# A new order for the first steps of a retention and gated feed-forward kernel, with filler products and two held-back loads

## The chip, the cores and the metric

The kernel runs on one core of a Trainium2 chip. The metric is the device time of one execution in microseconds (us); the runs are repeated, and the median counts. Smaller is better.

## What is computed

The reference has two parts in sequence, all in float32:

```python
# q, k, v: (B=4, H=8, S=768, D=64); gamma: one constant per head
for t in range(S):
    state = gamma * state + outer(k[:, :, t], v[:, :, t])      # (B, H, D, D)
    y[:, :, t] = (1 / sqrt(D)) * q[:, :, t] @ state
x = y.transpose(0, 2, 1, 3).reshape(3072, 512)
h = x @ w_in                                                   # (512, 2048)
g = h * sigmoid(1.702 * h)
out = g @ w_out                                                # (2048, 512)
```

The kernel receives both weights as pairs of 32-bit words of 64-bit numbers, and narrows them to float32 by itself. Reading them so is part of its work, and most of the early work of VectorE.

## The kernel before, in words

**Attention.** The recurrence is done in chunks of 64 positions, for two batch entries at a time, so that there are 24 steps; the first eight (`2 * CB`) are written out in a list together with the first feed-forward block. For step j:

- `load` (L125 to L164) fetches q, k and v of the chunk. Steps 0 to 5 fetch them in plain form and turn them on TensorE. q and v come by SP's queue; k comes by the engine that the argument at L150 chooses: ACT for step 0, POOL for the others. q, k and v have two buffers each.
- `turn` (L241) makes eight transposes on TensorE (L250, four of q and four of k) into two PSUM tiles, and `turned` (L258) has ACT copy them to SBUF (L261).
- `decay` (L263) has ACT scale k by the decay within the chunk, one head at a time (L272, eight instructions).
- `attend` (L281) has two halves. Written `stepJ`, it makes the 16 products of k and q of step j (L289), into the tile `pa`. Written `step-F`, it makes the products of step f that need them: 16 of decayed k and v (L297, the addition to the state), 16 of the old state and q (L306, not for step 0), 16 of the masked product and v (L312). `pa` has one buffer, so the next `stepJ` waits until `masked` and `updated` have read it.
- `masked` (L316, L318) multiplies by the decay mask on VectorE. `by_state` ("state", L325), `output` ("x", L347, or L349 on ACT for a first chunk), `aged` (L357, ACT) and `updated` (L366 or L368, VectorE) make the output X and the new state.

**Feed-forward.** `up0` (L407) is a unit of 16 products of 128x128 by 128x256 in two groups of eight (L414; each product is seen twice in the profile[...]). "up0.T.P" takes the half T of the first block of positions and the P-th pair of columns of w_in. It needs X of steps 2T and 2T+1 and the P-th narrowed weights. "gate" is ACT's activation (L393) of the result.

**Narrowing.** `fetch` (L178) reads half a pair of columns, 512 KB, into one of three raw buffers by SP's queue (L180). `Narrow.start` ("abs", ACT, L207), `half` (three VectorE instructions, L211 to L213) and `rest` (three more, L217, L218, L222) make float32 of it. Weights 0 are done in two parts, 0a and 0b, and the others in one part of 1024 columns. A raw buffer is free after `rest`.

**Order.** A planner does not decide here. The list of names at the end (L944 to L962) is the program's order, and `pin` keeps it so on each engine: every name emits its instructions to its engines in the order of the list. Each engine runs in order and waits by semaphores. A DMA of SP's queue also waits for the one eight places before it to land. `begin` (L841) fetches small constants by POOL and makes the identity; `rows` (L859) and "mask" (L901) make the decay mask, and `causal` (L864) has POOL cut it to a triangle. `keep_warm` ("warm", L854) is a product of the identity by itself, 512 columns, into the spare PSUM tile `idle`. `lay_rowd` (L869) and `lay_whole` (L874) lay out more constants.

After the list comes the rest of the kernel: the blocks of positions after the first two, and the output products. The change does not touch it.

Of the kernel before, what the change touches and what calls it, by code (L numbers as in the profile page):

```python
# [9 lines left out]
F32 = mybir.dt.float32  # L10
# [3 lines left out]
P = 128  # L14
# [14 lines left out]
def kernel(  # L29
# [29 lines left out]
    pe, act, dve, pool, sp = nc.tensor, nc.scalar, nc.vector, nc.gpsimd, nc.sync  # L59
    ctx.enter_context(tc.manual_schedule(engines={mybir.EngineType.PE}))  # L60

    B, H, S, D = q.shape
    NT, DM = out.shape
    DFF = moe_w_in.shape[1]
    HP = H // 2
# [17 lines left out]
    ps_a = ctx.enter_context(tc.tile_pool(name="ps_a", bufs=1, space=bass.MemoryType.PSUM))  # L83
# [17 lines left out]
    rowd = const.tile([P, HP, D], F32, name="rowd")  # L101
# [3 lines left out]
    whole = const.tile([P, HP], F32, name="whole")  # L105
    whole_h = const.tile([P, H], F32, name="whole_h")
    ident = const.tile([P, P], F32, name="ident")
    mask = const.tile([P, 2, HP, D], F32, name="mask")
# [9 lines left out]
    def pin(i):  # L118
        return tc.keep_in_program_order(i) if ordered[0] else i
# [5 lines left out]
    def load(j, what="qkv"):  # L125

        b, c = j // NC * 2, j % NC
        rows = slice(c * D, (c + 1) * D)  # L130
        keep = tc.keep_in_program_order if j < 2 * CB else lambda i: i

        def plain(name, src, tag, bufs, engine=sp):
            t = two.tile([P, H, D], F32, name=name + "_in", tag=tag, bufs=bufs)
            QKV[name, j] = t
            for i in range(2):
                if j < NEW:
                    to, at = t[i * D:(i + 1) * D], src[b + i, :, rows, :].rearrange("h p d -> p h d")
                    for n in range(1 if name == "v" else 2):
                        keep(engine.dma_start(*((to, at) if name == "v" else (to[:, n:H:2], at[:, n * HP:(n + 1) * HP]))))  # L140
                else:
                    for r in range(2):
                        keep(engine.dma_start(t[r * D:(r + 1) * D, i * HP:(i + 1) * HP],
                                              src[b + i, r * HP:(r + 1) * HP, rows, :].rearrange("h p d -> p h d")))

        if j < NEW:
            if "q" in what:
                plain("q", q, "q_sq", 2)
            if "k" in what:
                plain("kn", k, "k_sq" if j in (0, 1, 4, 5) else "o", 2, pool if j else act)  # L150
        elif "q" in what:
            for name, src in (("q", q), ("k", k)):
                t = two.tile([P, H, D // C4, C4], F32, name=name + "_sq")
                for r0 in range(0, P, C4):
                    for n in range(D // C4):
                        t0 = c * D + n * C4
                        tc.keep_in_program_order(sp.dma_start(
                            t[r0:r0 + C4, :, n], src[b + r0 // D, :, t0:t0 + C4, r0 % D:r0 % D + C4]
                            .rearrange("h p d -> p h d")))
                QKV[name, j] = t  # L160
        if "v" in what:
            if j >= NEW and c < NC - 1:
                plain("kn", k, "kn", 1)
            plain("v", v, "v", 2)  # L164
# [4 lines left out]
    RAWS = [r.rearrange("p a b -> p (a b)").bitcast(U32)  # L169
            for r in (W2[:, 4], W2[:, 5], G[:, 6:8].rearrange("p a s t -> p a (s t)"))]  # L170
# [11 lines left out]
    class Narrow:  # L182
# [30 lines left out]
            pin(dve.scalar_tensor_tensor(hi, hi, 0x80000000, mu, op0=ALU.bitwise_and, op1=ALU.bitwise_or))  # L213

        def rest(self):
            m, mu, lo, hi = self.m, self.mu, self.lo, self.hi
            pin(dve.tensor_scalar(mu, hi, 0xFF800000, None, op0=ALU.bitwise_and))  # L217
            pin(dve.scalar_tensor_tensor(lo.bitcast(F32), lo, 2.0 ** -52, m, op0=ALU.mult, op1=ALU.mult))  # L218
            a, b = lo.bitcast(F32), hi.bitcast(F32)
            if self.i < NFF:  # L220
                a, b = [t.rearrange("p (c ab f) -> p c ab f", ab=2, f=P) for t in (a, b)]
            pin(dve.tensor_add(self.w, b, a))  # L222
# [4 lines left out]
    QT, KT, KD, AT, TURNED, PA, PU, PY, SHARE = [{} for _ in range(9)]  # L227
    HALF = [slice(i * D, (i + 1) * D) for i in range(2)]
    TWO = [(i, r) for i in range(2) for r in range(2)]
# [11 lines left out]
    def turn(j):  # L241

        QT[j], KT[j] = home(j, "qT"), home(j, "kT")
        if j < NEW:

            x = QKV.pop(("q", j)), QKV["kn", j]
            TURNED[j] = p = [ps.tile([P, HP, P], F32, name="pt", tag="y") for i in range(2)]
            for n in (1, 0) if j else (0, 1):
                for s in range(HP):
                    pe.matmul(p[n][:, s, :], x[n][:, 2 * s:2 * s + 2].rearrange("p r d -> p (r d)"), ident, is_transpose=True)  # L250
        else:
            for t, name in ((QT[j], "q"), (KT[j], "k")):
                tc.keep_in_program_order(dve.transpose(
                    t.rearrange("p h t -> p (h t)"), QKV.pop((name, j)).rearrange("p h n d -> p (h n d)")))
        if 2 * CB <= j < NCH - 2:
            load(j + 2, "qk")
# [386 lines left out]
    def down49(m, ring, comps):  # L643
# [25 lines left out]
        def home2(name, first, rest):  # L669
            kept[name] = first.rearrange("p (j e) -> p j e", e=P), rest[:, 0:3 * P].rearrange("p (j e) -> p j e", e=P)  # L670
            return kept[name]
# [167 lines left out]
    first = const.tile([P, 1], F32, name="first")  # L839
    idle = ps.tile([P, 4 * P], F32, name="idle", tag="x")  # L840
    works, products = {}, {}  # L841
# [12 lines left out]
    def keep_warm():  # L854

        pe.matmul(idle.rearrange("p (a b) -> p a b", a=4), ident, ident[:, None, :].to_broadcast([P, 4, P]),
                  start=True, stop=True)

    def rows():  # L859

        products["rows"] = p = ps.tile([P, H, D], F32, name="rows", tag="x")
        pe.matmul(p.rearrange("p h t -> p (h t)"), ones, row.rearrange("p h t -> p (h t)"), start=True, stop=True)
# [22 lines left out]
    def halves_anew():  # L885
# [14 lines left out]

        "mask": lambda: pin(dve.tensor_mul(m3, products["rows"], cold[:, 0:H, None].to_broadcast([P, H, D]))),  # L901
        "causal": causal, "rows": rows,
        "rowd": lay_rowd, "whole": lay_whole, "late_loads": late_loads, "anew": halves_anew,
        "warm": keep_warm}
    for j in range(2 * CB):
        for name in "qkv":
            works[f"{name}{j}"] = lambda j=j, name=name: load(j, name)
# [13 lines left out]
        works[f"w{i // 2}{'ab'[i % 2]}"] = lambda i=i: fetch(i)  # L921
    for name, i in [("0a", 0), ("0b", 1)] + [(str(p), 2 * p) for p in range(1, NFF)]:
        n = Narrow(i)
        works |= {"abs" + name: n.start, "half" + name: n.half, "rest" + name: n.rest}

    units = [0]

# [14 lines left out]

    begin()
    for name in """  # L944
        k0 table q0 warm turn0 w0b rows warm k1 abs0b q1 turned0 step0 v0 w0a half0b mask k2 turn1 causal rest0b
        masked0 decay0 v1 decay1 abs0a half0a step-0 updated0 turned1 q2 step1 rowd whole w2b turn2 w2a x0 k3
        aged1 masked1 turned2 v2 rest0a abs2 q3 step-1 updated1 state1 decay2 aged2 step2 q4 x1 half2 decay3 w3b
        w3a up0.0.0 masked2 turn3 k4 step-2 v3 q5 rest2 k5 gate0.0.0 turned3 updated2 state2 step3 up0.0.2
        masked3 abs3 half3 x2 rest3 turn4 w1b step-3 aged3 gate0.0.2 turned4 state3 w1a w5b updated3 v5 decay4
        abs1 x3 turn5 half1 up0.0.3 turned5 up0.1.2 step4 aged4 w5a rest1 v4 gate0.0.3 decay5 w6a masked4  # L950
        gate0.1.2 abs5 w6b step5-4 half5 rest5 up0.0.1 updated4 abs6 state4 gate0.0.1 w4b
        up0.1.1 half6 aged5 w4a up0.0.5 rest6 masked5 up0.1.5 gate0.1.1 x4 gate0.0.5 abs4 step-5 w8b w8a
        half4 gate0.1.5 state5 updated5 anew q6 up0.1.6 x5 rest4 gate0.1.6 abs8 v6 decay6 aged6 up0.0.6 w7b w7a half8
        turn6 gate0.0.6 up0.1.0 abs7 seven_4.2 seven_6.2 half7 gate0.1.0 w9b w9a up0.1.4 q7 gate0.1.4 step6 masked6 rest7 up0.0.4 v7
        gate0.0.4 seven_52.2 turn7 up0.1.3 gate0.1.3 step7-6 seven_4.0 masked7 updated6 decay7 aged7 abs9 state6 x6 up0.0.7 rest8 seven_w.0 gate0.0.7
        w11a w11b step-7 state7 x7 seven_x half9 w10b w10a up0.1.7 gate0.1.7
        seven2.0 seven2.1 abs11 rest9 seven2.2 seven_v.0 w12a w12b seven2.3 half11 seven2.4 abs10 seven_4.1 seven_w.1
        seven2.5 rest11 seven2.6 w14b w14a seven0.0 seven0.1 half10 seven0.2 abs12 seven0.3 rest10 w13a w13b seven0.4
        seven_v.1 seven0.5 seven_4.3 half12 seven_w.3 seven0.6 seven1.0 abs14 seven1.1 rest12 w15a w15b seven1.2 seven1.3
        half14 seven1.4 abs13 seven_v.3 seven1.5 updated7 rest14 seven1.6 seven3.0 seven3.1 half13 seven3.2 abs15 seven3.3  # L960
        rest13 seven3.4 seven3.5 late_loads half15 rest15 seven3.6 seven_end
    """.split():  # L962
        works[name]()
# [94 lines left out]
```

## Time and profile before

| | before |
|---|---|
| median of three runs, us | 661.88 (661.77 to 662.99) |
| the profiled execution, us | 662.24 |
| its span in the profile, us | 660.5 |
| mean granted clock of TensorE | 0.997 |
| TensorE busy with products, us | 642.2 (97%) |
| TensorE busy with weight loads, us | 580.2 (88%) |
| VectorE busy, us | 453.9 (69%) |
| ScalarE (ACT) busy, us | 159.0 (24%) |
| GpSimd (POOL) busy, us | 198.8 (30%) |

The span runs from the first to the last instruction of the program; the time of an execution is 1.74 us more in the profiled one. Shares of the span are averages over stages with different limits: the part that the list writes out runs to about 160 us, and attention steps 0 to 5 lie in its first 75 us. Times below are counted from the span's start. In a line of the timeline the first number is the start, the second the length of a group of instructions, in brackets stands the idle time before it and what ended it.

### The profile page before, as it was taken

What the parts mean: (1) busy time and instruction counts of PE and PEld (TensorE: products, weight loads), DVE (VectorE), ACT (ScalarE), POOL (GpSimd) and SP (SyncE); (2) the same over time, 40 slices, a digit from 0 to 9 for tenths busy, and PEclk for the clock granted to TensorE, in tenths of its full rate; (3) what the DMA queues carried; (4) which work ended last, traced back from release to release, by engine and by line L of the source; (5) the groups of instructions that cost most, each with busy time, mean ns of one, the idle gap of its engine ahead of it and who ended that gap; (6) DMA issues with size and microseconds to landing.
All of it is one profiled execution on the core that took longest, in us unless ns stands there. A gap on an engine that the chain in (4) does not pass through costs nothing.

```text
span 660.5 us, 15291 instructions
## 1 busy us (share of the span) xinstructions
PE 642.2 (97%) x6390; PEld 580.2 (88%) x6390; DVE 453.9 (69%) x645; ACT 159.0 (24%) x306; POOL 198.8 (30%) x225
## 2 busy tenths in 40 slices
PE   6789999999999999999999999999999999999997
PEld 3778888888788888889999888999888999988997
DVE  3699989999936973556984445995354995254965
ACT  4674233551000000333100233010233110233110
POOL 6400311310379217000536400445600255500000
PEclk9989999999999999999999999999999999999999
DMA  9995549763233556262485832386742252602142
GB/s 176 193 274 173 152 104 241 172 163 60 49 82 135 137 149 153 58 248 96 118 199 134 279 57 97 86 223 135 225 118 97 66 154 104 235 21 96 55 154 96
DMA packets 148149, 91.86 MB, mean 139 GB/s; under 512 B 131600, under 2 KB 134416, under 8 KB 147056
## 3 DMA queue, kind: packets, MB, share of 16 engines
q1 hardware_dynamic: 135856, 45.19, 29.8%
q0 software_dynamic: 9888, 44.46, 20.6%
q10 hardware_dynamic: 2336, 1.25, 0.6%
q8 instruction: 50, 0.82, 0.5%
q14 instruction: 19, 0.16, 0.1%
HBM read 72.89 MB, written 15.47 MB: 134 GB/s over the span
## 4 chain that ended last, share of the span: by engine, by line
PE 89%; DVE 4%; DMA 4%; SPq 1%; issue 1%; ACT 0%; DVEq 0%
PE pq L666 27%; PE px L562 17%; PE pd L799 13%; PE py L562 13%; PE ph L491 7%; PE ph L414 5%; PE pa L289 2%; PE py L312 2%; PE pa L297 2%; PE py L306 2%; DMA W<-in_moe_w_in_dram 1%; DMA W<-in_moe_w_out_dram 1%; DMA q_in<-in_q_dram 1%; PE pt L250 1%; SPq L140 1%
## 5 line engine op out<-in xcount | busy, mean ns | idle before, releaser
L635 POOL DMA_DIRECT2D ring<-W2D x28 | 15.4, 551 | 227.7 <-PE px L562 118.3
L666 PE MATMUL pq<-W,G 128*128 128x128 f32 x672 | 80.2, 276 | 0.0
L666 PEld LDWEIGHTS pq<-W,G 128*128 128x128 f32 x672 | 77.6, 192 | 1.3 <-issue 0.7
L666 PE MATMUL pq<-ring,own 128*128 128x128 f32 x448 | 60.1, 276 | 1.3 <-issue 1.3
L562 PE MATMUL px<-X,W1A 128*128 128x256 f32 x256 | 59.8, 379 | 0.0
L562 PE MATMUL px<-X,W1B 128*128 128x256 f32 x256 | 59.8, 379 | 0.0
L666 PEld LDWEIGHTS pq<-ring,own 128*128 128x128 f32 x448 | 54.5, 192 | 0.4
L562 PEld LDWEIGHTS px<-X,W1B 128*128 128x128 f32 x256 | 48.5, 190 | 6.7
L562 PEld LDWEIGHTS px<-X,W1A 128*128 128x128 f32 x256 | 48.4, 190 | 6.5
L393 ACT ACTIVATE G<-G 128x512 f32<-128x512 f32 x60 | 37.4, 628 | 54.7 <-DVE G L572 33.4
L799 PE MATMUL pd<-W,G 128*128 128x256 f32 x224 | 49.6, 381 | 0.0
L799 PEld LDWEIGHTS pd<-W,G 128*128 128x128 f32 x224 | 42.2, 190 | 5.9
L562 PE MATMUL py<-X,W1A 128*128 128x256 f32 x192 | 45.4, 379 | 0.0
L562 PE MATMUL py<-X,W1B 128*128 128x256 f32 x192 | 45.4, 379 | 0.0
L562 PEld LDWEIGHTS py<-X,W1A 128*128 128x128 f32 x192 | 36.5, 190 | 5.0
L562 PEld LDWEIGHTS py<-X,W1B 128*128 128x128 f32 x192 | 36.5, 190 | 5.0
L580 DVE TENSOR_TENSOR t<-py,u 128x512 f32<-128x512 f32 x16 | 11.1, 692 | 32.3 <-PE py L562 32.3
L569 ACT ACTIVATE p<-px 128x512 f32<-128x512 f32 x16 | 9.6, 597 | 96.0 <-PE px L562 96.0
L414 PE MATMUL ph<-X,W1A 128*128 128x256 f32 x128 | 30.6, 397 | 0.9 <-DVE X L347 0.9
L594 DVE TENSOR_TENSOR G<-G 128x512 f32<-128x512 f32 (+2 forms) x24 | 12.3, 513 | 25.7 <-ACT G L393 25.7
L666 PE MATMUL pq<-ring,G 128*128 128x128 f32 x224 | 29.6, 275 | 0.0
L666 PE MATMUL pq<-W,own 128*128 128x128 f32 x224 | 29.6, 275 | 0.0
(237 smaller groups left out, 1226.0 us busy)
## 6 DMA issues: line engine op xcount, KB each, us to landing
ring<-W2D POOLq DMA_DIRECT2D x28, 768.0 KB, 4.8
W1B<-W1D POOLq DMA_DIRECT2D x6, 1792.0 KB, 9.8
W<-in_moe_w_in_dram SPq DMA_DIRECT2D x12, 512.0 KB, 5.9
W<-in_moe_w_out_dram SPq DMA_DIRECT2D x10, 512.0 KB, 5.8
out_dram<-o POOLq DMA_DIRECT2D x20, 256.0 KB, 3.0
q_sq<-in_q_dram SPq DMA_DIRECT2D x144, 32.0 KB, 2.1
k_sq<-in_k_dram SPq DMA_DIRECT2D x144, 32.0 KB, 2.1
v_in<-in_v_dram SPq DMA_DIRECT2D x72, 64.0 KB, 3.1
```

What stands on the lines that cost most here:

```text
L289: pe.matmul(pa[HALF[w], u, 0, s, :], kt[HALF[u], w, s, :], qt[HALF[u], w, s, :], start=True, stop=True)
L297: pe.matmul(pa[HALF[u], w, 1, s, :], kd[HALF[w], HP * u + s, :], vn[HALF[w], HP * u + s, :], start=True, stop=True)
L306: pe.matmul(py[HALF[o], u, 1, 2 * w + s2, :], old[HALF[u], w, 2 * s2 + o, :], qt[HALF[u], w, 2 * s2 + o, :], start=True, stop=True)
L312: pe.matmul(py[HALF[o], w, 0, 2 * u + s2 if f < NEW else 2 * s2 + u, :], vn[HALF[w], HP * u + s, :], a[HALF[w], u, s, :], start=True, stop ...
L393: pin(act.activation(g, h[:, i], AF.Gelu_apprx_sigmoid))
L414: pe.matmul(h[:, ab], w, X[:, 2 * th + c // 2, c % 2, :], start=(ab == 0 and c == 0), stop=(c == 3), skip_group_check=True)
L491: pe.matmul(acc[:, u, :], w, x, start=(start and u == 0 and c == 0), stop=(stop and c == 1), skip_group_check=True)
L562: pe.matmul(acc[:, u, :], t[:, q1 + u, sa, c, :], X[:, sb, c, :], start=(start and u == 0 and c == 0), stop=(stop and c == 1), skip_group_ ...
L594: dve.tensor_sub(q[0][1], q[0][0], q[0][1])
L635: pool.dma_start(c, W2D[i])
L666: pe.matmul(p0[:, j, :], a[:, d], w[:, d], start=(new and j == 0 and d == 0), stop=(d == NP // 2 - 1), skip_group_check=True)
L799: pe.matmul(p0[:, n, :], g1(m, p, sa)[:, n * P:(n + 1) * P], W2[:, sb, p, :], start=(new and p == 0 and n == 0), stop=(last and p == NP - ...
```

## The change

Four functions are new. `prime` makes 28 products of 64x64 with the identity on both sides, into the tile `pa` ahead of step 0, and nothing reads them. `tick` is a product of the identity with 128 columns into `idle`. `hold_w2` writes one word of the third raw buffer on VectorE, so that the fetch into its first half (w2a) waits for that. `hold_k2` copies one column of the masked product of step 0 on POOL, so that what follows on POOL's queue, the k of steps 2 and 3, waits for `masked0`. k of steps 4 and 5 is fetched by SP instead of POOL. `rest` is split in two, so that other VectorE work can stand between its parts. The list is reordered from its start to the first step 6, and "q7" moves ahead of step 6's decay. No arithmetic of the result is left out or added.

```diff
-                plain("kn", k, "k_sq" if j in (0, 1, 4, 5) else "o", 2, pool if j else act)
+                plain("kn", k, "k_sq" if j in (0, 1, 4, 5) else "o", 2, (act, pool, pool, pool, sp, sp)[j])
...
         def rest(self):
+            self.resta()
+            self.restb()
+
+        def resta(self):
             m, mu, lo, hi = self.m, self.mu, self.lo, self.hi
             pin(dve.tensor_scalar(mu, hi, 0xFF800000, None, op0=ALU.bitwise_and))
             pin(dve.scalar_tensor_tensor(lo.bitcast(F32), lo, 2.0 ** -52, m, op0=ALU.mult, op1=ALU.mult))
-            a, b = lo.bitcast(F32), hi.bitcast(F32)
+
+        def restb(self):
+            a, b = self.lo.bitcast(F32), self.hi.bitcast(F32)
...
+    def prime():
+
+        p = ps_a.tile([P, 2, 2, HP, D], F32, name="pa", tag="pa")
+        for s in range(7):
+            for u, w in TWO:
+                pe.matmul(p[HALF[w], u, s // HP, s % HP, :], ident[HALF[u], 0:D], ident[HALF[u], 0:D], start=True, stop=True)
+
+    def hold_w2():
+        pin(dve.memset(RAWS[2][0:1, 0:1], 0))
+
+    def hold_k2():
+        pin(pool.tensor_copy(first, AT[0][:, 0, 0, 0:1]))
+
+    def tick():
+
+        pe.matmul(idle[:, 0:P], ident, ident, start=True, stop=True)
...
-        k0 table q0 warm turn0 w0b rows warm k1 abs0b q1 turned0 step0 v0 w0a half0b mask k2 turn1 causal rest0b
-        masked0 decay0 v1 decay1 abs0a half0a step-0 updated0 turned1 q2 step1 rowd whole w2b turn2 w2a x0 k3
-        aged1 masked1 turned2 v2 rest0a abs2 q3 step-1 updated1 state1 decay2 aged2 step2 q4 x1 half2 decay3 w3b
-        w3a up0.0.0 masked2 turn3 k4 step-2 v3 q5 rest2 k5 gate0.0.0 turned3 updated2 state2 step3 up0.0.2
-        masked3 abs3 half3 x2 rest3 turn4 w1b step-3 aged3 gate0.0.2 turned4 state3 w1a w5b updated3 v5 decay4
-        abs1 x3 turn5 half1 up0.0.3 turned5 up0.1.2 step4 aged4 w5a rest1 v4 gate0.0.3 decay5 w6a masked4
-        gate0.1.2 abs5 w6b step5-4 half5 rest5 up0.0.1 updated4 abs6 state4 gate0.0.1 w4b
-        up0.1.1 half6 aged5 w4a up0.0.5 rest6 masked5 up0.1.5 gate0.1.1 x4 gate0.0.5 abs4 step-5 w8b w8a
-        half4 gate0.1.5 state5 updated5 anew q6 up0.1.6 x5 rest4 gate0.1.6 abs8 v6 decay6 aged6 up0.0.6 w7b w7a half8
-        turn6 gate0.0.6 up0.1.0 abs7 seven_4.2 seven_6.2 half7 gate0.1.0 w9b w9a up0.1.4 q7 gate0.1.4 step6 masked6 rest7 up0.0.4 v7
+        k0 table q0 warm prime turn0 w0b rows tick tick k1 abs0b q1 mask turned0 step0 v0 half0b hold_w2 causal turn1 w0a decay0
+        resta0b masked0 v1 decay1 turned1 restb0b whole hold_k2 k2 w2b w2a tick tick step-0 updated0 step1 q2 abs0a x0 masked1
+        half0a v2 rowd aged1 w3b k3 tick tick step-1 resta0a state1 x1 restb0a updated1 q3 w3a abs2 v3 tick tick tick
+        up0.0.0 gate0.0.0 half2 turn2 turned2 decay2 aged2 resta2 w1b w1a step2 masked2 restb2 k4 q4 step-2 state2 x2
+        updated2 abs3 half3 up0.0.2 gate0.0.2 v4 w5b w5a turn3 turned3 decay3 resta3 step3 masked3 aged3 restb3 k5 q5
+        step-3 up0.0.3 state3 x3 updated3 abs1 gate0.0.3 half1 v5 turn4 turned4 w6b w6a decay4 rest1
+        up0.1.2 gate0.1.2 step4 abs5 masked4 aged4 up0.0.1 half5 gate0.0.1 w4b w4a turn5 turned5 rest5 abs6 up0.1.1
+        decay5 gate0.1.1 step5-4 half6 masked5 state4 updated4 up0.0.5 aged5 rest6 gate0.0.5 x4 up0.1.5 abs4 gate0.1.5
+        step-5 w8b w8a half4 state5 updated5 anew q6 up0.1.6 x5 rest4 gate0.1.6 abs8 w7b w7a v6 q7 decay6 aged6 up0.0.6
+        half8
+        turn6 gate0.0.6 up0.1.0 abs7 seven_4.2 seven_6.2 half7 gate0.1.0 w9b w9a up0.1.4 gate0.1.4 step6 masked6 rest7 up0.0.4 v7
```

More of the change, by code (lines that the diff above doesn't have):

```diff
@@ L903 @@
         "rowd": lay_rowd, "whole": lay_whole, "late_loads": late_loads, "anew": halves_anew,
-        "warm": keep_warm}
+        "warm": keep_warm, "tick": tick, "prime": prime, "hold_w2": hold_w2, "hold_k2": hold_k2}
     for j in range(2 * CB):
@@ L923 @@
         n = Narrow(i)
-        works |= {"abs" + name: n.start, "half" + name: n.half, "rest" + name: n.rest}
+        works |= {"abs" + name: n.start, "half" + name: n.half, "rest" + name: n.rest,
+                  "resta" + name: n.resta, "restb" + name: n.restb}
     units = [0]
```

## The prediction

> **What bounds the kernel now.** I read the page first (shares of busy time and the 40 slices), then the table of stretches over the first 105 us, then the timeline of the same part, engine by engine.
>
> ```profile
> PE 642.2 (97%) x6390; PEld 580.2 (88%) x6390; DVE 453.9 (69%) x645; ACT 159.0 (24%) x306; POOL 198.8 (30%) x225
> ...
> PE   6789999999999999999999999999999999999997
> ...
> DVE  3699989999936973556984445995354995254965
> ```
>
> TensorE (PE) is busy for 642.2 of 660.5 us. A slice is 16.5 us: what PE leaves idle is nearly all in the first three, so the change can win only there, up to about 56 us, and VectorE (DVE) is full from the third slice on: PE can't run ahead of it for long. Stretches (busy time of PE, its weight loads, DVE, ACT, POOL; then granted clock, DMA share, GB/s):
>
> ```profile
> 3.90:26.70 22.80, 18.91 (x270) 12.93 (x274) 10.56 (x18) 12.20 (x33) 15.41 (x25) 1.00 1.14 213
> ...
> 33.50:36.96 3.46, 1.63 (x85) 1.46 (x78) 3.13 (x5) 2.60 (x6) 0.00 (x0) 1.00 1.21 294
> 36.96:40.37 3.41, 3.41 (x9) 2.71 (x9) 3.34 (x5) 1.55 (x5) 0.00 (x0) 0.50 0.89 223
> ...
> 56.00:69.90 13.90, 13.90 (x71) 12.08 (x64) 13.56 (x17) 4.19 (x9) 0.40 (x1) 1.00 0.51 137
> ```
>
> Until 26.70 DMA is saturated (share over 1) and DVE idles half the time; from 56 PE has no gap. In between, PE was idle for half of 33.50:36.96 and then got half its clock for 3.41 us. The timeline shows what held the first steps:
>
> ```profile
> 12.62 1.13 PE L289 MATMUL pa<-G 64*64 64x64 f32 x32
> ...
> 17.60 0.66 ACT L207 ACTIVATE W1A<-W 128x512 f32<-128x512 f32 x1 [2.08 <-DMA W<-in_moe_w_in_dram]
> ...
> 18.29 0.43 DVE L211 TENSOR_SCALAR W1A<-W1A 128x512 f32<-128x512 f32 x1 [2.25 <-ACT W1A L207]
> ...
> 19.92 0.68 DVE L366 COPY state<-pa 128x512 f32<-128x512 f32 x1
> ...
> 20.75 1.13 PE L289 MATMUL pa<-G 64*64 64x64 f32 x32 [2.62 <-DVE state L366]
> ...
> 28.09 2.21 PE L414 MATMUL ph<-X,W1A 128*128 128x256 f32 x9 [0.94 <-DVE X L347]
> ...
> 36.07 0.69 PE L289 MATMUL pa<-G 64*64 64x64 f32 x32 [1.83 <-DVE state L368]
> ```
>
> L289 is the first part of an attention step. That of step 1 (20.75) waits for the copy at L366, which stands in DVE's order behind three operations on weights that had not landed (17.60). So a late weight transfer holds the attention chain. The same L289 takes 1.13 at 12.62 and 20.75, 0.69 at 36.07: until about 26.7 PE runs at half speed, though the clock column shows 1.00 there.
>
> [...] The trace[...] shows that half an idle window (1.63 of 3.46 busy) suffices for the loss. [...]no wait of PE in the trace is clearly one for instructions. [...]
>
> **The change, part by part** (times from the span's start).
>
> *Prime.* 28 products of 64x64 after the idle one, an untried number in an existing form: 16 such took 1.06 to the next start (L289 at 12.62, half clock), so 28 take 1.9, 5.95 to 7.8; bounds 1.0 (full clock, 0.6 per 16) and 2.1. The first transposes could begin at 6.72 (q's landing), so 1.1 lands on PE's path: transposes 7.8 to 9.7, rows (2.0) to 11.7 instead of 10.6, two ticks (a quarter of 2.0 each) to 12.7, step 0 at 12.75 (before 12.62, when ACT's evictions end). In return PE has no gap from 3.9 to about 13.8[...]. A gain below nothing is possible if the clock isn't granted sooner; if it is granted about 10, rows end some 0.9 sooner.
>
> *Mask first, weights second on DVE.* Mask 11.8 to 12.5 (0.69); POOL's two selections (1.85) to 14.4; half0b 1.55, to 14.1; hold_w2 a memset (0.06 to 0.17 in the rows at L851 and L852), 14.2; resta0b 0.42+0.86 to 15.5; masked0 to 16.2 (before 16.05). Step -0 at 16.3. Then L366 follows it at once, 17.45 to 18.15, no longer behind w0a: step 1 at 18.25, against 20.75, **2.5 sooner**. ACT is ready: 16 decays (3.9) and two evictions from 11.7 make 16.7.
>
> *To the first unit.* Step 1 to 19.35, masked1 20.05, half0a 21.7 (w0a landed at 17.57 before, not later now), resta0a 22.9, state1 and x1 24.3, restb0a 25.0: unit 0.0.0 at 25.1 against 28.09, **3.0 sooner**. updated1 25.7.
>
> *Steps 2 and 3, now each in one piece* (turn, step, step -, one unit). half2 (0.69+0.69+1.23) to 28.3. PE: unit 3.44, to 28.5 (16 halves of 0.215); turn2 0.9, 29.4; ACT's eviction of two halves 1.1 behind the gate, 30.3; step2 30.9; ACT's eight decays 2.0, 32.3; step -2 to 33.3. DVE: resta2 (1.9) 30.2, masked2 31.6, restb2 32.8, so unit 0.0.2 runs 33.3 to 36.7; before 36.70 to 41.7, with turn3 and step3 already done. Likewise DVE's state2, x2, updated2 (2.1), half3 (2.6), resta3 (1.9), masked3: 40.6; step -3 to 42.1; unit 0.0.3 42.1 to 45.5. Then turn4, unit 0.1.2, step 4: 50.4; rest1 is through DVE at about 50. Unit 0.0.1 to 53.8, turn5 0.9, unit 0.1.1 3.4, step 5-4 1.9, units 0.0.5 and 0.1.5 6.9: 66.9, where before stood at 70.0. **3.1 sooner**, and DVE about as much (rest6 at 64.4 against 67.2).
>
> *Holds and queues.* k2 goes out on POOL after masked0, about 16.6 to 19.1 instead of 6.2 to 8.7; with the 5.3 to 7.7 that k3 took there it lands by 26.8, needed at 28.5: hidden by 1.7; bounds 0 and 2. hold_w2 stops SP at its second half of w2 until 14.2; q2, v2 and w3b stand behind it. q2 moves past two transfers of 512 KB, 1.7 each at about 300 GB/s (294 in the stretch from 33.50), and lands about 23, needed at 29: nothing. hold_k2's copy (0.74 at most, L890) keeps POOL from nothing but k2 and k3. k4 and k5 on SP cost it 8 issues of 0.65, beside other work: w5, behind q4, which now waits for turn2, goes out at about 34 and lands by 44 even with the longest 10.25 seen, needed about 51: nothing. Three more ticks before unit 0.0.0 fill idle time. No arithmetic is dropped.
>
> *Step 7's loads* stand on SP before w9, and w7 goes ahead of step 6's k and v.
>
> ```profile
> 94.13 0.69 PE L289 MATMUL pa<-G 64*64 64x64 f32 x32 [0.72 <-DVE G L253]
> ```
>
> This wait goes: **0.7**; bounds 0 and 1.1. Behind it PE is at work to 160 without a gap, so what is won is carried to the end.
>
> *Clock.* The new gaps (29.4 to 30.3, 30.9 to about 32; 37.6 to 38.5, 39.0 to 40.7; before unit 0.0.0 if PE is at full speed by then, about 2.6) invite the loss seen at 36.96. One stretch of 3.41 at half clock costs 1.7. Before's own is in its times, so each new one counts. I take one, 1.7; bounds 0 and 7. For the earlier grant I take the 0.9.
>
> *Sum:* 3.1+0.7+0.9-1.7 = 3.0 off the span of 660.5: 657.5. The profiled run took 662.24, 1.74 around its span, so 659.2 for it; the median of the runs shown, 661.88, lies 0.36 under that run: 658.9.
>
> **Rivals.**
> *Half clock in every gap (slower).* At all three places one or two windows are lost, 1.7 to 3.4 each, 5.1 to 10.2, middle 7.0; against 3.8 won: 3.2 slower, 665.1. It decides from a loss of 5.1, three windows. For it: the case at 36.96 needed only 1.8 of idling. Against: each new gap is broken by a short step[...].
> *Gain used up (no change).* Two such windows (3.4)[...]: 3.8-3.4 = 0.4, 661.5. For it: ACT's evictions and decays are now between PE's products with no unit to cover them.
> *Clock granted early and kept:* 3.8+0.9 = 4.7, 657.2. For it: PE without a gap from 3.9. Against: 9.65 to 13.07 was nearly full before and brought no grant.
>
> **How the numbers follow.** Forecast 658.9: 0.47; early and kept 0.20; used up 0.15; slower 0.18. A measurement of this kernel tells 0.2% (1.3 us) from no change at best. Faster 0.66, same 0.15, slower 0.19. The range 655.6 to 663.4 covers the first three with the bounds of k2 and prime and the lighter part of the slower case.
>
> **What would show it.** Right: L366 straight behind step -0; step 1's L289 near 18; unit 0.0.0 near 25; step -5 near 67; no wait for L253 near 91; at most one stretch at 0.50. Wrong: several stretches at 0.50 before 50; transposes of step 2 waiting for k or q; PE idle over 3 us before 0.0.2 or 0.0.3; DVE's rest6 no sooner than 67.

## The result, and the profile after

| | before | after |
|---|---|---|
| median, us | 661.95 (659.48 to 664.85, 20 runs) | 665.25 (661.05 to 670.41, 20 runs) |
| ratio to before, 95% interval | | 1.0056 [1.0035, 1.0078] |
| the profiled execution, us | 662.24 | 661.14 |
| its span, us | 660.5 | 659.4 |
| mean granted clock, all runs | 0.996 | 0.994 |

The change makes the kernel slower by 0.6%, about 3.5 us; 658.9 was forecast, 3 us faster. Ratios and means here and below leave out five slow runs, each over 1.5% above the fastest of its kernel. The profiled execution of the changed kernel is one of its best: it took 1.1 us less than the profiled one of before. So its trace shows what the change can do, and where its lead goes, but not the whole of the median.

The page after, at the lines that were shown of before (from L225 on, a line of before has a number higher by 6 or more):

```profile
PE 638.3 (97%) x6462; PEld 578.9 (88%) x6462; DVE 452.0 (69%) x646; ACT 158.6 (24%) x306; POOL 199.0 (30%) x218
...
PE   6689999999999999999999999999899999999997
...
DVE  3888899999936963547984445985354995254965
```

72 more products are seen, the identity's for the most part, and VectorE (DVE) is busier in its second slice (8 for 6). In slice 29 of TensorE (PE) there is an 8 that before did not have, at 467 us, far behind the change. The stretches (columns as before):

```profile
3.90:26.70 22.80, 18.84 (x333) 14.83 (x334) 14.64 (x24) 11.87 (x32) 11.10 (x18) 0.93 1.16 225
8.19:11.61 3.42, 2.47 (x13) 1.35 (x11) 1.47 (x3) 1.52 (x3) 0.80 (x1) 1.00 1.32 184
11.61:15.02 3.41, 3.24 (x42) 3.12 (x43) 3.31 (x7) 3.41 (x16) 1.97 (x4) 0.50 1.20 236
...
56.00:69.90 13.90, 13.90 (x272) 12.00 (x270) 12.57 (x15) 7.20 (x20) 0.94 (x2) 1.00 0.64 170
```

The clock is granted at 8.2 instead of 26.7, taken back for one stretch of 3.41 (PE was idle for 0.95 us of the 3.42 ahead of it), and kept from 15.0 (mean 1.00 from 15.02 to 660). In the first stretch DVE does 14.64 us of work where it did 10.56. The timeline, all engines, first steps:

```profile
11.78 1.13 PE L295 MATMUL pa<-G 64*64 64x64 f32 x32 [1.12 <-ACT G L267]
...
16.11 0.69 DVE L372 COPY state<-pa 128x512 f32<-128x512 f32 x1 [0.64 <-PE pa L303]
...
16.95 0.69 PE L295 MATMUL pa<-G 64*64 64x64 f32 x32 [0.44 <-DVE state L372]
...
23.43 3.69 PE L420 MATMUL ph<-X,W1A 128*128 128x256 f32 x16 [2.04 <-DVE W1A L228]
...
33.57 3.72 PE L420 MATMUL ph<-X,W1A 128*128 128x256 f32 x16 [1.52 <-DVE X L353]
```

Step 1 (L295, 16.95) comes 3.8 us sooner than before, unit 0.0.0 (23.43) 4.7, unit 0.0.2 (33.57) 3.1. At step -5 (L303, 68.35; before 70.03) 1.7 is left. Then PE's timeline at steps 6 and 7:

```profile
93.09 0.69 PE L295 MATMUL pa<-G 64*64 64x64 f32 x32 [1.37 <-DVE G L259]
...
99.73 0.70 PE L303 MATMUL pa<-v_in,G 64*64 64x64 f32 x31 [0.89 <-POOL G L280]
...
104.91 1.46 PE L497 MATMUL ph<-W,W1B 128*128 128x256 f32 x6
```

The next stage (L497) begins at 104.91, and before it began at 104.92: in 37 us the whole lead of 1.7 is gone, nearly all of it (1.5) in the two waits in brackets: the first is 0.65 longer than before's 0.72, and the second is new. What stands behind them is in the queues. SP's timeline, each group one load (number of its DMAs at the end):

```profile
75.09 0.90 SPq L180 DMA_DIRECT2D W<-in_moe_w_in_dram  x2
76.04 2.60 SPq L143 DMA_DIRECT2D kn_in<-in_k_dram  x4
78.73 2.57 SPq L143 DMA_DIRECT2D v_in<-in_v_dram  x4
81.35 4.05 SPq L157 DMA_DIRECT2D q_sq<-in_q_dram  x8
85.50 5.14 SPq L157 DMA_DIRECT2D k_sq<-in_k_dram  x8
90.68 0.92 SPq L180 DMA_DIRECT2D W<-in_moe_w_out_dram  x2
91.70 2.58 SPq L143 DMA_DIRECT2D kn_in<-in_k_dram  x4
```

and SP's longest wait between 60 and 106:

```profile
SPq L180 <- DVE W1B L228: 6.8, 1, 6.8
```

SP stood 6.8 us at the weights 7 (L180), until DVE had freed their buffer at 75.1 ("rest4"). Behind it stood kn and v of step 6, q and k of step 7, the weights 9 and kn of step 7, and from there SP issues without a pause to 98. What follows on POOL and on DVE:

```profile
82.07 1.45 POOL L280 TENSOR_TENSOR G<-kn_in,cold 128x512 f32<-128x512 f32 x1 [6.31 <-DMA kn_in<-in_k_dram]
83.49 1.48 POOL L365 TENSOR_TENSOR state<-state,whole_h 128x512 f32<-128x512 f32 x1
...
97.96 1.72 POOL L280 TENSOR_TENSOR G<-kn_in,cold 128x512 f32<-128x512 f32 x1 [12.99 <-DMA kn_in<-in_k_dram]
```

```profile
81.93 0.69 DVE L211 TENSOR_SCALAR W1B<-W1B 128x1024 f32<-128x1024 f32 x1 [1.24 <-ACT W1B L207]
82.66 1.41 DVE L212 TENSOR_SCALAR W1B<-W1B 128x1024 uint32<-128x1024 uint32 x1
84.10 1.95 DVE L213 SCALAR_TENSOR_TENSOR W<-W,W1B 128x1024 uint32<-128x1024 uint32 x1
...
91.03 0.71 DVE L259 STREAM_TRANSPOSE G<-q_sq 128x512 f32<-128x512 f32 x1
92.23 0.71 DVE L259 STREAM_TRANSPOSE G<-k_sq 128x512 f32<-128x512 f32 x1 [0.49 <-DMA k_sq<-in_k_dram]
```

The decay of step 6 on POOL (82.07; before 77.52) now runs beside DVE's narrowing of the weights 7. There L212 and L213 take 1.41 and 1.95, where they take 0.69 and 1.23 with POOL at rest (at 76.34 and 77.07). Before had the same overlap, one narrowing sooner, at the weights 8:

```profile
78.02 1.41 DVE L212 TENSOR_SCALAR W<-W 128x1024 uint32<-128x1024 uint32 x1
```

In after DVE gets through the weights 8 undisturbed (L213 takes 1.23 at 77.07), but then stands idle for 1.24 until ACT has the weights 7 (81.93), and there L212 and L213 take 1.4 us more all the same. So step 7's transposes of q (L259, 91.03; before 91.49) come 0.5 sooner than before, while PE is 1.7 sooner. With 0.49 more for k, PE waits 1.37. The decay of step 7 starts at 97.96 (before 96.09), though its kn was asked for at 91.70, as before (91.53): the transfer and the operation took longer here (6.26 us from the asking to the start, before 4.56; the operation 1.72, before 1.04), and PE, which now needs the result sooner, waits 0.89. The lead of 1.7 us is worth nothing here, where the loads are not sooner too.

### The profile page after: what moved, and what is told of

Read it like the earlier page. It is cut to its first block, busy times and chain, and to the rows that moved or that the text cites. A ratio compares the mean times of both kernels' runs of the same rounds, so it can differ in the third digit from the quotient of the medians.

```text
span 659.4 us, 15432 instructions
## 1 busy us (share of the span) xinstructions
PE 638.3 (97%) x6462; PEld 578.9 (88%) x6462; DVE 452.0 (69%) x646; ACT 158.6 (24%) x306; POOL 199.0 (30%) x218
## 4 chain that ended last, share of the span: by engine, by line
PE 86%; DMA 5%; DVE 2%; SPq 2%; POOL 2%; ACT 1%; issue 1%; POOLq 0%; ACTq 0%; DVEq 0%
PE pq L672 25%; PE px L568 17%; PE pd L805 15%; PE py L568 12%; PE ph L497 6%; PE ph L420 4%; PE pa L295 2%; PE py L318 1%; PE pa L303 1%; PE py L312 1%; SPq L157 1%; DMA whole<-in_col_decay_dram 1%; DMA kn_in<-in_k_dram 1%; DMA G<-in_moe_w_out_dram 1%; DMA k_sq<-in_k_dram 1%
## 5 line engine op out<-in xcount | busy, mean ns | idle before, releaser
L399 ACT ACTIVATE G<-G 128x512 f32<-128x512 f32 x60 | 37.4, 628 | 54.9 <-DVE G L578 33.4
L805 PE MATMUL pd<-W,G 128*128 128x256 f32 x224 | 49.6, 381 | 0.0
L805 PEld LDWEIGHTS pd<-W,G 128*128 128x128 f32 x224 | 42.2, 190 | 5.8
L420 PEld LDWEIGHTS ph<-X,W1A 128*128 128x128 f32 x128 | 23.8, 190 | 7.5 <-ACT W1A L207 2.2
L672 PE MATMUL pq<-W,own 128*128 128x128 f32 x224 | 29.6, 275 | 0.0
```

The costliest lines, as they stand in the source:

```text
L399: pin(act.activation(g, h[:, i], AF.Gelu_apprx_sigmoid))
L420: pe.matmul(h[:, ab], w, X[:, 2 * th + c // 2, c % 2, :], start=(ab == 0 and c == 0), stop=(c == 3), skip_group_check=True)
L672: pe.matmul(p0[:, j, :], a[:, d], w[:, d], start=(new and j == 0 and d == 0), stop=(d == NP // 2 - 1), skip_group_check=True)
L805: pe.matmul(p0[:, n, :], g1(m, p, sa)[:, n * P:(n + 1) * P], W2[:, sb, p, :], start=(new and p == 0 and n == 0), stop=(last and p == NP - ...
```

## The experiments

All ratios are to the kernel before on the same chip. "Lost clock" is one minus the mean granted clock, times 660 us; one stretch of 3.41 us at half clock is 1.7 us of it. A start at half clock does not count in it: the clock record begins at 26.72 in before and at 8.20 in after, and ahead of that the column shows 1.00. For the changed kernel the two rows together give 1.0054.

| kernel | ratio | 95% interval | lost clock, us |
|---|---|---|---|
| before (137 runs) | 1 | | 2.7 |
| after | 1.0056 | [1.0035, 1.0078] | 4.2 |
| after, again | 1.0052 | [1.0024, 1.0079] | 4.3 |
| 128-column fill | 1.0067 | [1.0043, 1.0090] | 2.6 |
| weights 7 last | 1.0152 | [1.0105, 1.0198] | 8.1 |
| no identity products | 1.0099 | [1.0066, 1.0131] | 2.8 |
| kn and v of step 6 first | 1.0003 | [0.9985, 1.0021] | 4.4 |
| before + identity products | 1.0047 | [1.0029, 1.0065] | 5.9 |
| no holds | 1.0065 | [1.0036, 1.0094] | 5.4 |
| order alone | 1.0100 | [1.0077, 1.0122] | 6.1 |
| step 6 first + 512-column fill | 0.9975 | [0.9959, 0.9991] | 0.8 |
| step 6 first + one gap filled | 0.9994 | [0.9975, 1.0013] | 3.4 |
| order of before behind step -5 | 0.9998 | [0.9980, 1.0015] | 2.5 |
| k of steps 4 and 5 on POOL | 1.0073 | [1.0049, 1.0097] | 4.2 |

**The changed kernel once more.** No edit.

> The changed kernel unaltered, for the clock and span of each of its executions and for another profile. Half-clock theory: time falls with the mean granted clock, about 1.7 us for each 0.0026 of it (one stretch of 3.41 us at half clock in 660), from about 661 at 0.997 to 670 at 0.987; and a profile of a slow execution shows several stretches at 0.50 before 60 us, in or behind the gaps of steps 2 and 3, with the same instructions running twice as long. Rival (loads or instruction fetch make the spread): the time does not go with the clock, and a slow profile shows a longer wait for a DMA.

1.0052: the loss repeats. Its profiled execution (span 662.8) had one stretch at half clock, at 12.2, as the first had, and is still 3.4 us longer. PE's waits in it:

```profile
PE pa L295 <- ACT G L267: 3.2, 3, 1.6
PE px L568 <- POOL X L538: 2.6, 1, 2.6
...
PE pa L295 <- DVE G L259: 1.9, 1, 1.9
PE pd L805 <- DVE W1B L554: 1.2, 2, 0.9
```

The wait at step 7 (L259) is there again, 1.9. Up to 175 us this execution is 0.5 behind the first. Of the rest, 2.1 is lost on PE near 180 (L805, of which the profile shows 1.2 as waits) and 0.9 at the longer wait near 467 (L538). The wait near 180 is in 11 of the 14 profiles of this study, before's too, and is missing in the first profile of after: no part of the change, but a reason why that profile flatters it.

The granted clock alone hardly makes the loss: in executions with a mean clock of 0.996 to 0.998 this kernel took 664.5 on average (4 executions), and before, on the same chip, 661.5 (15). At 0.999 or more it took 662.1 (5, with those of the first 20), and before 661.4 (21 on all chips), too few to tell.

**Gaps filled with 128-column products.**

```diff
+    def fill(n, tag):            # n identity products into a tile of their own
...
-resta2 w1b w1a step2 masked2
+resta2 w1b w1a fill3 step2 fill3 masked2
-half3 up0.0.2
+half3 fill5 up0.0.2
-resta3 step3 masked3
+resta3 fill3 step3 fill3 masked3
-v3 tick tick tick
+v3 tick tick tick tick tick tick
```

> Identity products of 128 columns are added in the gaps: 3 more before unit 0.0.0, 3 before and 3 behind step 2 and step 3 each, 5 before unit 0.0.2. Half-clock theory: median 661 to 662.5, the slow executions of 666 to 670 gone, mean clock 0.994 or more in nearly all. Rival (the gaps themselves or late loads cost the time): no change of the median of about 665, or up to 2 us slower, since the added products delay the steps.

The lost clock falls from 4.3 to 2.6 us, and the time does not: 1.0067. The trace of PE shows one price:

```profile
32.84 0.56 PE L318 MATMUL py<-G,v_in 64*64 64x64 f32 x18 [2.02 <-issue]
```

In the middle of a group of products PE had nothing to do for 2.02 us and waited for no engine; 1.7 us earlier a block of instructions had come in (in the trace's packets its transfer ran from 29.77 to 31.16). That the idle time was a wait for this block is not shown. And the wait for L259 was 1.7 here, too: what the head had won would have been given back there anyway. Which of the two kept the time up is not told apart.

**The weights 7 behind q of step 7.**

```diff
-abs8 w7b w7a v6 q7 decay6
+abs8 v6 q7 w7b w7a decay6
```

> Only the loads of step 7 move: v6 and q7 stand ahead of w7b and w7a in the list, so that they don't wait behind the fetch of weights 7, which waits for rest4. Theory that the lead of the first steps is given back there: the waits of 1.37 before step 7 and 0.89 before step -7 go, 1 to 2 us faster than the changed kernel, in all its executions alike, so a spread of the same width. Half-clock theory alone: no change, about 665.

1.0152: the opposite of what was expected. ACT, in its timeline:

```profile
90.80 1.12 ACT L207 ACTIVATE W1B<-W 128x1024 f32<-128x1024 f32 x1 [10.22 <-DMA W<-in_moe_w_in_dram]
91.82 0.38 ACT L399 ACTIVATE W1A<-ph 128x256 f32<-128x256 f32 x1
```

The 16 issues of q and k of step 7 (8 us) now stood ahead of the weights 7, which went out at 85.42; ACT waited 10.22 us at the first step of their narrowing, and the gate (L399) for which PE waited was behind it. PE stood idle for 5.05 us, and its clock was halved from 90.6 to 97.4. So the weights must not go last either; the kernel after the next lets what can go at once go first.

**No identity products.** `prime` and all ticks taken out (one 512-column product is left, where before had two).

> The changed order and the two holds without prime and without the ticks. If prime and ticks help (clock granted sooner): slower by 1 to 3 us, 666 to 668. If they do harm, because an early grant is what the gaps then take back: 0 to 2 us faster than the changed kernel, 663 to 665, at a mean clock that hides it since a start at half clock is not in the record.

1.0099, with the first grant at 29.6: in the new order the products are worth some 0.45% (1.0099 against 1.0054, give or take 0.37), with little of it in the clock.

**kn and v of step 6 first.**

```diff
-abs8 w7b w7a v6 q7 decay6
+abs8 v6 w7b w7a q7 decay6
```

> The changed kernel with one edit behind step -5: kn and v of step 6 are asked for ahead of the weights 7 again, as before (abs8 v6 w7b w7a q7 decay6). Theory 1, the lead of 1.7 us that step -5 has is given back in SP's queue: in the changed kernel SP stands 6.8 us at the weights 7 until DVE has freed W1B at 75.1, and kn and v of step 6, q and k of step 7 and kn of step 7 are issued behind it one after the other until 94.3. With kn and v of step 6 ahead, their 5.2 us of issuing lie inside that wait; the wait for the transposes of step 7 near 93 (1.4 us) and the one for kn of step 7 near 99.7 (0.9) shrink, and the median falls by 1.2 to 2.3 us to 663 to 664.5. Theory 2, the loss is the clock of the first 45 us: the profile changes near 93 as said, and the median stays at 665 to 666.5 with the mean clock still 0.992 or 0.993.

1.0003: 0.0053 (give or take 0.0028) or 3.5 us less than the changed kernel, more than the 1.2 to 2.3 expected, with the clock as bad as there (4.4 us lost). At a mean clock of 0.996 to 0.998 it took 658.0 (5 executions), before on the same chip 659.8 (12). SP, POOL and PE in its trace:

```profile
69.51 3.52 SPq L143 DMA_DIRECT2D kn_in<-in_k_dram  x4
73.12 2.58 SPq L143 DMA_DIRECT2D v_in<-in_v_dram  x4
75.80 1.06 SPq L180 DMA_DIRECT2D W<-in_moe_w_in_dram  x2
```

```profile
76.32 1.36 POOL L280 TENSOR_TENSOR G<-kn_in,cold 128x512 f32<-128x512 f32 x1
...
93.55 1.04 POOL L280 TENSOR_TENSOR G<-kn_in,cold 128x512 f32<-128x512 f32 x1 [14.43 <-DMA kn_in<-in_k_dram]
```

```profile
92.13 0.69 PE L295 MATMUL pa<-G 64*64 64x64 f32 x32
...
97.81 0.69 PE L303 MATMUL pa<-v_in,G 64*64 64x64 f32 x32
...
102.92 3.40 PE L497 MATMUL ph<-W,W1B 128*128 128x256 f32 x15
```

The eight DMAs of kn and v fill the time that SP stood still, the weights 7 go out 0.7 later than they did, and the loads behind them 3.3 to 4.6 us sooner. Both brackets are gone, and the next stage begins at 102.92, 2.0 us sooner. Over all profiles: with the order of the change behind step -5 PE waits 1.0 to 1.9 us for L259 near 93 (seven profiles), with the same head and kn and v of step 6 first 0 to 0.4 (four). With before's own order the wait is 0.7, and 1.3 in the kernel that follows here: the order of the loads is not the only thing that makes it.

**Before, with the identity products alone.**

```diff
-q0 warm turn0 w0b rows warm k1
+q0 warm prime turn0 w0b rows tick tick k1
-half0a step-0
+half0a tick tick step-0
-q3 step-1
+q3 tick tick step-1
-w3a up0.0.0
+w3a tick tick tick up0.0.0
```

> The kernel before, with the identity products alone added: 28 small ones ahead of the first transposes, two in place of the second warm-up and seven more ahead of step -0, step -1 and unit 0.0.0; its own order, no holds, its own queues for k. Theory 2 (an early clock is taken back in the gaps that follow): the mean clock falls from 0.996 towards 0.992, and the median rises by 1 to 2 us to 663 to 664. Rival, the identity products are worth something by themselves (without them the changed kernel is 2 us slower) and the order is what costs: the median falls by 0.5 to 2 us to 660 to 661.5, and the first steps run at the full clock from about 9 us.

1.0047, lost clock 5.9: that an early clock is taken back (theory 2) holds for the old order. In its trace, PE and then the stretches:

```profile
20.36 1.13 PE L295 MATMUL pa<-G 64*64 64x64 f32 x32 [3.43 <-DVE state L372]
...
29.18 0.38 PE L295 MATMUL pa<-G 64*64 64x64 f32 x9 [2.49 <-issue]
```

```profile
14.56:17.98 3.42, 1.16 (x64) 1.05 (x64) 1.26 (x3) 1.43 (x5) 3.42 (x6) 1.00 1.36 217
17.98:24.80 6.82, 4.43 (x68) 4.12 (x72) 4.64 (x8) 4.49 (x11) 4.31 (x8) 0.50 1.12 243
```

PE is early and finds the weights' wait that was there anyway (3.43 where it was 2.62), the stretch with 1.16 of 3.42 busy is followed by 6.8 us at half clock, and a wait of 2.49 marked "issue" comes on top. How the 3 us lost divide among the three was not tried.

**No holds**, and **the order alone** (no identity products, no holds, k of steps 1 to 5 on POOL).

```diff
-half0b hold_w2 causal
+half0b causal
-whole hold_k2 k2
+whole k2
```

> The changed kernel without the two holds (the memset ahead of the second weights, the copy on POOL ahead of k of step 2). If the holds do what they are for, the transfers that step 0 and step 1 wait for land later, step 1 comes 0.5 to 1.5 us later, and the median is 666 to 667.5. If the holds cost (POOL stands at its hold with the constants of L915 and k behind it), the median falls to 664 to 665. If they do nothing, 665.3 to 666.4 as the changed kernel had.

> The new order alone: the changed kernel without the identity products, without the holds, and with k of steps 1 to 5 on POOL as before. If the order costs by itself, 666 to 669 (the order with holds and queues, without the products, had 667.9). If it is the holds and the queues of k that cost, 661 to 664, near the kernel before.

Without the holds 1.0065, which the intervals do not tell from 1.0054. Step 1 comes at 16.31, 0.6 sooner than with them (16.95), where 0.5 to 1.5 later was expected: that they bring the first transfers forward is not shown. In the middle of step -1 PE stood idle for 4.17 us, the longest wait marked "issue" of the study,

```profile
22.24 1.02 PE L303 MATMUL pa<-v_in,G 64*64 64x64 f32 x28 [4.17 <-issue]
```

and the transfer of a block of instructions ran from 19.19 to 20.66. The two profiles of the changed kernel have no such wait above 0.2, but others with the holds have (1.5 with kn and v of step 6 first, 2.0 with the 128-column fill): it is not shown that the holds prevent it. The order alone, 1.0100, is as slow as the order with holds and queues but without products. In all of these step 7's loads still wait, so that what a head of 1 or 2 us wins would hardly show.

**Step 6 first, and the gaps filled with few instructions**; **the same with one gap filled.**

```diff
-rows tick tick k1
+rows tick tick warm k1
-v3 tick tick tick
+v3 tick tick tick warm warm
-resta2 w1b w1a step2
+resta2 w1b w1a warm step2
-half3 up0.0.2
+half3 warm up0.0.2
```

The second has eight more ticks ahead of unit 0.0.0 instead.

> The version that asks for kn and v of step 6 first, with five more 512-column products of the identity, each in a gap of the first 35 us: one behind the mask's product, two ahead of unit 0.0.0, one ahead of step 2, one ahead of unit 0.0.2. Theory 2 as it stands now: that version loses 4.4 us of the granted clock on average (mean clock 0.9933 in 22 runs) where the kernel before loses 2.6 (0.996), because windows behind those gaps are granted half. With the gaps filled by few instructions the mean clock rises to 0.996 or more and the median falls by 1 to 2 us against the same version without them, to about 0.997 of the kernel before (658 to 659.5). If the gaps aren't what costs clock, the clock stays at 0.993 and the ratio at 1.000. If more instructions on PE bring waits for instructions (as with the 128-column fill), the clock rises and the ratio still is 1.000 or more.

> The version that asks for kn and v of step 6 first, with eight more 128-column products (1.8 us at full clock) in one place alone, the gap of 2.3 us ahead of unit 0.0.0. In its profile the half-clock stretch followed that gap (23.3 to 26.7). If that gap is the one that costs clock, the mean clock rises from 0.9933 to about 0.995 and the ratio falls to 0.998; if all gaps share in it, 0.999 to 1.000.

With five 512-column products the lost clock falls from 4.4 to 0.8 us and the ratio to 0.9975: faster than before, and 0.0028 (give or take 0.0024) or some 1.9 us better than without them. One gap alone gives about a third of both, in time within its error. Stretches of the version without the fill, laid on the windows of its own clock record (3.41 us each, counted from the first grant):

```profile
16.48:19.90 3.42, 2.83 (x136) 2.46 (x131) 2.45 (x5) 1.70 (x5) 3.42 (x7) 1.00 1.16 286
19.90:23.31 3.41, 1.18 (x29) 0.92 (x18) 3.31 (x7) 2.30 (x5) 1.62 (x3) 1.00 1.27 177
23.31:26.72 3.41, 3.36 (x8) 2.76 (x9) 3.31 (x5) 0.00 (x0) 0.00 (x0) 0.50 1.13 208
```

and with it:

```profile
20.68:24.10 3.42, 2.90 (x11) 1.52 (x11) 3.39 (x6) 1.15 (x1) 0.87 (x1) 1.00 1.21 187
```

The gap ahead of unit 0.0.0 left PE busy for 1.18 of a window, and the unit behind it ran at half clock; filled to 2.90, it keeps the clock. The profiled execution of the filled version is one of its worst (664.58): it stood idle for 3.2 us (3.19, marked "issue") inside L318 until 34.81, at the same place in PE's instructions (the trace has 961 loads and products ahead of it) as the 128-column fill. Two windows at half clock followed (34.3 to 41.2).

**The order of before behind step -5**, ahead of it the changed one; and **k of steps 4 and 5 on POOL** in the changed kernel.

```diff
-abs8 w7b w7a v6 q7 decay6 aged6 up0.0.6 half8
+abs8 v6 decay6 aged6 up0.0.6 w7b w7a half8
...
-up0.1.4 gate0.1.4
+up0.1.4 q7 gate0.1.4
```

```diff
-(act, pool, pool, pool, sp, sp)[j]
+(act, pool, pool, pool, pool, pool)[j]
```

> The changed kernel up to step -5, the order of the kernel before from there (kn and v of step 6, then decay 6 and unit 0.0.6, then the weights 7; q of step 7 behind the weights 9). If theory 1 holds, it is as good as the version that only asks for kn and v of step 6 first: ratio 0.998 to 1.003, no wait near 93. If the gain of that version came from elsewhere, it stays with the changed kernel at 1.005 or more.

> The changed kernel with k of steps 4 and 5 on POOL as before in place of SP. These are eight issues of some 0.65 us, which in SP's queue lie ahead of the weights 5 and 6 and of the loads behind them; if SP's queue is short of time already in steps 3 to 5, the ratio falls from 1.005 to 1.002 or less. If it is short only behind step -5, no change: 1.004 to 1.007. If POOL has no time for them (it has the decays and states), 1.008 or more.

0.9998: with before's order behind step -5 the loss is gone as well, and the wait near 93 is 0.2. 1.0073: the queue of k of steps 4 and 5 makes no difference that can be told, with the same reservation as for the holds.

## Why the prediction was wrong

**The first steps** came as worked out, or sooner: step -0 at 15.35 (16.3), L372 straight behind it, step 1 at 16.95 (18.25), unit 0.0.0 at 23.43 (25.1), unit 0.0.2 at 33.57 (33.3), unit 0.0.3 at 42.07 (42.1). Step -5 was put at about 67 and came at 68.35. So the lead of 3.1 was down to 1.7 there: PE's own work between unit 0.0.3 and step -5, in which it hardly waits (0.3), had come out 1.4 short in the sum.

**Step 7's loads: the step that failed.** "This wait goes: 0.7; bounds 0 and 1.1." It said that q of step 7 stands ahead of the weights 9 and "w7 goes ahead of step 6's k and v", and priced the second at nothing. It was a wait moved ahead of eight DMAs that could have gone out meanwhile, kn and v of step 6, for SP did not pass the weights 7 before rest4 (it stood 6.8 us there); the 26 DMAs behind them came late with them. In the trace the wait grew from 0.72 to 1.37, one of 0.89 came new, and the lead of 1.7 was zero at 104.9. Undone alone it is worth 3.5 us (0.0053 of the time, give or take 0.0028), as much as the whole loss, and the wait of 0.72 then falls to between 0 and 0.4, so that half or more of the 0.7 forecast here does come. The traces show 2.0 of the 3.5 at 102.9 and 2.7 at 111. A further 1.4 is the wait for L538 near 467, 0.3 there and 1.7 in after. There, too, POOL waits for a kn from SP; that this follows from the same lateness was not tried, and waits for L538 of up to 2.0 us come in another order as well.

**"Behind it PE is at work to 160 without a gap, so what is won is carried to the end."** With kn and v of step 6 first it held: PE waits for nothing from 93 to 160. In after it did not: the 0.89 at 99.7 and one of 0.45 at 112.4 (L497, for ACT) came new. Beyond, the waits near 180 and 467 take or give up to 2 us in single executions, and the first of them differs with no part of the change.

**Clock: a term that was sized too small.** One stretch at half clock was taken, 1.7, in a sum whose steps otherwise run at full clock. Over all runs after loses 4.3 us, two and a half stretches; before loses 2.7. Among before's 137 runs the time hardly follows the clock (0.2 us for each us lost); among 35 of after it does (0.8). That is an association and no proof, and why before differs is not shown. Filling the gaps is the test: with five products 3.6 us less clock is lost and 1.9 us of time is won, though the interval leaves it open whether that is 0.3 or 3.4. In the two profiles of after the lost stretch is not at the gaps of steps 2 and 3, as the prediction had it: it is the second window after the grant, and the windows over those gaps (1.7 to 2.7 us busy) keep the clock. In other kernels with this head a stretch is lost there.

The rival that had this as its cause, half clock in every gap, was right on the sign, and its 665.1 lies beside the 665.25 measured by luck. It decides from 5.1 us lost, and 4.2 was lost on average; and the loss of time goes away with the clock left as it was. What it and the forecast have in common, that gaps cost clock, is right (4.4 us lost with kn and v of step 6 first, 0.8 with the gaps filled).

**Prime and ticks** were given 0.9 for the earlier clock. They are worth some 3 us in the new order (1.0099 without, 1.0054 with, give or take 2.4) and cost 3 in the old one: they can't be priced by themselves. That it depends on whether the next work is ready fits the wait of 3.43 above, and was not tried apart.

**Holds and queues: nothing.** As put, within the errors: k on SP or POOL and the holds make no difference that can be told, in an order whose later wait would hide a small one.

Together the terms come near the 6.4 us between forecast and median: 3.5 for step 7's loads, 1.4 for PE's work up to step -5, and as an estimate from the figures above (0.5 to 0.8 us of time for each us of clock) 1.4 to 2.1 for the 2.6 us of clock lost beyond the one stretch. With the failed step put right, the forecast is still not met: the median is then that of before (1.0003), not 3 us under it. Its one profile, with a span of 655.3, is one of the best of its 22 executions and lacks the wait near 180.

## What to carry to other kernels

When a load moves up in a queue that issues in order, look at what it waits for and at all that it then holds up (SP stood 6.8 us here, with 26 DMAs behind): put first what can go at once. Here one swap of names in a list decided over some 3.5 us, about as much as the change was meant to win. A lead won early has to be followed through each later place where a transfer, not an engine, sets the time: here 1.5 of the lead of 1.7 us went in two such waits. And a gap that PE gains by being early can have a price in clock: in the old order a stretch with PE busy for 1.16 of 3.42 us was followed by 6.8 us at half clock. Five wide instructions in such gaps won 1.9 us here, behind loads put right; many small ones won nothing, but ahead of loads that were not.

## What the runs showed of the hardware

- PE's four longest waits marked "issue" (2.0, 2.5, 3.2 and 4.2 us, in four kernels) each end 1.4 to 1.7 us after the transfer of a block of instructions (16,384 bytes) has ended: at 32.84 against 31.16 with the 128-column fill, at 22.24 against 20.66 without the holds. Two of them, and a shorter one of 1.4 us in the version with one gap filled, stand at the same place in PE's instructions, behind 961 loads and products, though the programs differ there. In three of the four kernels the stretch around the transfer had DMA at a share of 1.10 to 1.26 (1.16 with the 128-column fill, 24 to 30; 1.10 with the five products, 26.75 to 34.30; 1.26 without the holds, 18 to 24). That PE waits for these blocks is not shown: in the first profile of after 51 packets came on the instruction queue, and its longest wait marked "issue" is 0.2.
- The same operation on DVE (L212, 128x1024) takes 0.69 us with POOL at rest (0.86 once, in before at 113.69) and 1.41 beside POOL's decay, and POOL's decay takes 1.04 to 1.72. In after the three operations that overlapped end as follows: L212 ended at 84.07, and POOL's end at 83.52 plus the 0.69 of L212 at rest is 84.21; POOL's L365 ended at 84.97, and 84.07 plus 1.04, its length in before at 97.09 (L359 there), is 85.11; L213 ended at 86.05, and 84.97 plus the 1.23 of L213 at rest is 86.20. Each comes 0.14 or 0.15 sooner than a full wait for the other engine's end would have it; what makes them so long is not shown. In after POOL's decay stood beside L212 after 6.31 us of waiting for a late kn, and DVE, which doesn't need that kn, took 1.4 us more for L212 and L213.
- PE's busy time in the windows that kept the clock and in those that lost it can be read from the traces, if stretches are laid on each profile's own clock record: 3.41 us each, counted from the first grant (26.72 in before, 8.20 in after; the one stretch at half clock is 3.41 us long in both). In the 14 profiles, over the first 26 windows and without the first of each, every one of the 13 full-clock windows followed by half clock had PE busy for at most 1.58 us, and every one of the 314 that kept it for at least 1.64. In before it is one window (1.58) against 23 (2.52 the least), in the first profile of after none against 24 (1.83 the least). The nearest two of the 14 profiles, of before and of after once more:

```profile
33.55:36.96 3.41, 1.58 (x81) 1.41 (x74) 3.08 (x5) 2.55 (x6) 0.00 (x0) 1.00 1.21 294
```

```profile
90.73:94.15 3.42, 1.64 (x8) 1.11 (x6) 2.53 (x5) 0.66 (x2) 0.00 (x0) 1.00 0.68 185
```

The first window after the first grant is different: 2.15 to 2.50 us did not keep the clock there in five profiles (after's 2.46, from 8.20 to 11.61, among them; nor did 1.24 in a sixth), 2.68 and more kept it in seven, and before's 2.47 kept it as well; why is open. In the kernels with early identity products the first grant came at 7.0 to 9.9 us, 8.20 in the first profile of after. That windows counted from there cut the same gap differently from execution to execution would explain why the lost clock varies so much between executions of one kernel; it was not tried.
